# 64-token chunks scored in 64x64 array tiles, y kept transposed, and the attention of 256 tokens traced pair by pair among the MLP of older tokens

## The chip, the cores and the metric

One Trainium2 chip, one of its cores. The metric is the device time in microseconds of one execution, the median of three runs. The profile is one execution's, taken by the hardware profiler.

## What is computed

A gated recurrence (HGRN2) for 4 sequences of 768 tokens with 8 heads of 48 features, then an MLP with the quick GELU on the 3072 tokens. The weights come as float64, all else as float32; everything is computed in fp32.

```python
f = 1 / (1 + exp(-f_logit))                       # [4, 8, 768, 48]
for t in range(768):
    state = f[:, :, t, :, None] * state + einsum('bhd,bhe->bhde', k[:, :, t], v[:, :, t])
    y[:, :, t] = einsum('bhd,bhde->bhe', q[:, :, t], state)
x = y.transpose(0, 2, 1, 3).reshape(3072, 384)
h = x @ w_in                                      # [384, 2048]
out = (h / (1 + exp(-1.702 * h))) @ w_out         # [2048, 384]
```

## The kernel before

`attention` (L136) does a pair of heads of one sequence, all 768 tokens at once, in six chunks of 128. Heads lie on partitions 0 to 47 and 64 to 111. q, k and the gate f are loaded token by token (L144), the gap between the heads is zeroed on GpSimd (L148), and TensorE turns them to [feature, token] (L159). Within a chunk a pair of tokens (s, t) is scored at the one level m = 1, 2, .. 64 at which s lies in the first and t in the second half of a block of 2m tokens. At each level ScalarE copies the second halves of q into a block-diagonal operand `qz` with zeros for the other head (L179), TensorE multiplies it with k for each chunk (L204; the diagonal, L186), VectorE writes the result under a mask into A (L208), and multiplies half of q and half of k by products of gates (L216, L217), which GpSimd makes (L219). Then k is turned back (L228), the states of the chunks are made (L233 into dS, L240), and y is summed from the state's part (L254) and A times v (L258), into `y_nat` [token, feature]. `turn` (L266) transposes that to xT once a sequence's four pairs are done.

`mlp_step` (L276) takes 384 tokens: 16 blocks of h (L284, three matmuls each), sigmoid on ScalarE (L288), product on VectorE (L289), and then three outputs of 16 matmuls (L293), copied (L298) and stored (L300).

`load_weights` (L95) takes 56 pieces. Each comes by DMA as the bits of float64 (L102) and is rounded to fp32 by ten VectorE and three GpSimd instructions (L111 to L130), in which the engines wait for each other twice.

The program traces the pairs of a sequence and then the MLP of the sequence before it. A scheduler then orders each engine's instructions by its own estimate of when they are ready; engines and SP's DMA queue execute in that order.

Of the kernel before, what the change touches and what calls it, by code (L numbers as in the profile page):

```python
# [10 lines left out]
I32 = mybir.dt.int32  # L11
AF = mybir.ActivationFunctionType
ALU = mybir.AluOpType


@with_exitstack
def kernel(
# [24 lines left out]
    C = 128                     # tokens of a chunk  # L42
    NCH = S // C                # chunks of a sequence
    NG = NCH // 2               # chunks of a PSUM bank
# [3 lines left out]
    HC = C // 2  # L48
    NK = DM // P
    NFF = DFF // P  # L50
    TM = S // 2                 # tokens of an MLP step
    FG = 4                      # blocks of d_ff in one tile of g
    assert S % C == 0 and C == P and NCH % 2 == 0 and DM % P == 0 and D <= HS
# [3 lines left out]
    att = ctx.enter_context(tc.tile_pool(name="att", bufs=3))  # L57
    wp = ctx.enter_context(tc.tile_pool(name="wp", bufs=2))
    mlp = ctx.enter_context(tc.tile_pool(name="mlp", bufs=2))
    ps = ctx.enter_context(tc.tile_pool(name="ps", bufs=2, space=bass.MemoryType.PSUM))  # L60
# [3 lines left out]
    # masks[s, l, t']: is s in the first half of the block of 2m tokens whose second half has the t'-th of  # L64
    # the chunk's second-half tokens?
    masks = const.tile([P, len(LEV), HC], F32, name="masks")
    nc.gpsimd.memset(masks, 1.0)
    for l, m in enumerate(LEV):
        blocks = HC // m
        for base, step, chan in ((0, -2 * m, 1), (m - 1, 2 * m, -1)):  # L70
            nc.gpsimd.affine_select(
                out=masks[:, l, :], in_=masks[:, l, :], compare_op=ALU.is_ge, fill=0.0, base=base,
                pattern=[[step, blocks], [0, m]], channel_multiplier=chan,
            )

    # Block-diagonal operands for two heads: the zeros stay, the blocks come and go.
    def diagonal(name, shape, n):
        tiles = [const.tile(shape, F32, name=f"{name}{j}") for j in range(n)]
        for t in tiles:
            nc.gpsimd.memset(t, 0.0)  # L80
        return cycle(tiles)

    qz = diagonal("qz", [P, 2, S // 2], 3)
    stz = diagonal("stz", [P, NCH - 1, 2, D], 2)

# [3 lines left out]
    WI, WO = 256, 192           # columns of a piece of w_in and of w_out  # L89
    pieces = [(w_in[:, c, f:f + WI], moe_w_in[c * P:(c + 1) * P, f:f + WI])  # L90
              for c in range(NK) for f in range(0, DFF, WI)]
    pieces += [(w_out[:, c, e:e + WO], moe_w_out[c * P:(c + 1) * P, e:e + WO])
               for c in range(NFF) for e in range(0, DM, WO)]

    def load_weights(n, dst, src):  # L95
        """One piece of w_in or w_out.  A float64 comes as its bits and is rounded to the nearest fp32."""
        w = dst.shape[1]
        if moe_w_in.dtype == F32:
            nc.sync.dma_start(out=dst, in_=src)
            return  # L100
        bits = wp.tile([P, w, 2], I32, tag="bits", name=f"bits_{n}")
        nc.sync.dma_start(out=bits.rearrange("p c two -> p (c two)"), in_=src.bitcast(I32))  # L102
        lo, hi = bits[:, :, 0], bits[:, :, 1]

        def tmp(tag, dtype=I32, nm=None):
            return wp.tile([P, w], dtype, tag=tag, name=f"{nm or tag}_{n}", bufs=1)
# [3 lines left out]
        e, over, fits = tmp("e"), tmp("over", F32), tmp("fits")  # L110
        ve.tensor_scalar(e, hi, 1, 21, op0=ALU.logical_shift_left, op1=ALU.logical_shift_right)  # L111
        po.tensor_scalar(over, e, 1151.0, 3.0e38, op0=ALU.is_ge, op1=ALU.mult)  # L112
        ve.scalar_tensor_tensor(fits, e, 897.0, over, op0=ALU.is_ge, op1=ALU.is_gt)
        # sign: the sign bit, and the bit by which the low 8 bits of the exponent field turn from one bias
        # to the other; as an fp32 it is 2 or -2.
        sign, t = tmp("sign"), tmp("t")
        ve.tensor_scalar(sign, hi, -(1 << 31), 1 << 30, op0=ALU.bitwise_and, op1=ALU.bitwise_xor)
        po.tensor_tensor(dst, over, sign.bitcast(F32), ALU.mult)
        # t: the value cut off after 23 bits of mantissa.
        ve.tensor_scalar(t, hi, 4, 1, op0=ALU.logical_shift_left, op1=ALU.logical_shift_right)  # L120
        ve.scalar_tensor_tensor(t, lo, 29, t, op0=ALU.logical_shift_right, op1=ALU.bitwise_or)  # L121
        ve.tensor_tensor(t, t, sign, ALU.bitwise_xor)
        # r: the 29 bits after those, times the power of two that they count from.
        r, p2 = tmp("e", nm="r"), tmp("sign", nm="p2")
        rf = r.bitcast(F32)
        ve.tensor_scalar(r, lo, (1 << 29) - 1, None, op0=ALU.bitwise_and)
        ve.tensor_scalar(p2, t, -(1 << 23), None, op0=ALU.bitwise_and)
        ve.scalar_tensor_tensor(rf, r, 2.0 ** -52, p2.bitcast(F32), op0=ALU.mult, op1=ALU.mult)  # L128
        po.tensor_tensor(rf, rf, t.bitcast(F32), ALU.add)  # L129
        ve.copy_predicated(dst, fits, rf)  # L130

    def halves(t, m):
        """[p, block of 2m, half, m] of a tile that holds the S tokens of a sequence."""
        return t.rearrange("p (n two m) -> p n two m", two=2, m=m)

    def attention(b, a, y_nat):  # L136
        i = f"{b}_{a}"
# [1 line left out]
        raw = {}  # L139
        for nm, src in (("f", f_logit), ("q", q), ("k", k), ("v", v)):  # L140
            w = D if nm == "v" else HS
            t = ld.tile([P, NCH, 2, w], F32, tag=f"{nm}raw", name=f"{nm}raw_{i}")
            for h in range(2):
                nc.sync.dma_start(  # L144
                    out=t[:, :, h, :D], in_=src[b, 2 * a + h].rearrange("(c p) d -> p c d", p=C)
                )
            if w > D:
                nc.gpsimd.memset(t[:, :, :, D:], 0.0)  # L148
            raw[nm] = t
        vv = raw["v"]  # L150

# [1 line left out]
        T = {}  # L153
        for nm in "fqk":
            t = att.tile([P, S], F32, tag=f"{nm}T", name=f"{nm}T_{i}")
            for c0 in range(0, NCH, NG):
                pt = ps.tile([P, NG, C], F32, tag="tr", name=f"tr_{nm}_{i}_{c0}", bufs=1)
                for c in range(NG):
                    nc.tensor.transpose(pt[:, c, :], raw[nm][:, c0 + c], ident)  # L159
                nc.scalar.activation(  # L160
                    t[:, c0 * C:(c0 + NG) * C], pt.rearrange("p c t -> p (c t)"),
                    AF.Sigmoid if nm == "f" else AF.Copy,
                )
            T[nm] = t
        Q, K, F = T["q"], T["k"], T["f"]

# [1 line left out]
        # The two heads of a pair share a product: K of both is stationary, and Q moves block by block,  # L168
        # each head's columns with zeros in the other's rows.
        A = att.tile([P, 2 * NCH, C], F32, tag="A", name=f"A_{i}", bufs=2)  # L170

        def blocks(src):
            z = next(qz)
            for h in range(2):
                rows = slice(h * HS, (h + 1) * HS)
                dst = z[rows, h, :src.free_size()]
# [169 lines left out]
```

## Time and profile before

| | |
|---|---|
| runs | 1086.9, 1084.12, 1085.43 us, median 1085.43 |
| profiled execution, first to last instruction | 1085.1 us |
| TensorE (PE) busy | 926.2 us, 4376 matmul records |
| VectorE (DVE) busy | 550.4 us |
| ScalarE (ACT) busy | 327.5 us |
| GpSimd (POOL) busy | 209.2 us |
| granted TensorE clock, mean | 0.909 |
| HBM read, written | 31.46 MB, 4.72 MB |

How to read it: a row of groups has line, engine, operation, output and inputs by the program's names, shapes and count, then the busy time in all and the mean ns of one, then the idle time of the engine before them and what ended it. PEld is the loading of the stationary operand, which goes on beside PE. PE rows count each fp32 matmul twice and a transpose once. Rows of the timeline merge like instructions that follow each other: start, time from the first's start to the last's end, count. A matmul's time includes its way through the array (222 ns for the smallest here), so matmuls that follow each other overlap in it.

### The profile page before, as it was taken

To read this page: it belongs to the slowest core of one execution; us is meant where nothing else is said; L and a number is where in the kernel's file an instruction comes from. 1 tells how busy PE (TensorE), PEld (TensorE's weight loads), DVE (VectorE), ACT (ScalarE), POOL (GpSimd) and SP (SyncE) were. 2 spreads that over 40 slices of the span, in tenths; PEclk is the share of its full clock that TensorE was granted. 3 is DMA by queue.
4 is the path that set the end of the run, shared out by engine and by line. 5 is a ranking of instruction groups with operands and counts; after the bars stand their busy time and mean duration, and the time that the engine had idled before them with its cause. 6 is when DMAs were issued, how large, how long until landed. Compare 5 with 4: busy or idle time off the path is not lost.

```text
span 1085.1 us, 12313 instructions
## 1 busy us (share of the span) xinstructions
PE 926.2 (85%) x4376; PEld 645.8 (60%) x4376; DVE 550.4 (51%) x1264; ACT 327.5 (30%) x705; POOL 209.2 (19%) x354
## 2 busy tenths in 40 slices
PE   4676675856748568999999999999999999999998
PEld 3475564534645446655577776655777766555554
DVE  3878769787777878220267546203575462021120
ACT  3243232412213214120444533204445432021110
POOL 5335143544445442000100110001100000000000
PEclk9768669777867869999999999999999999999999
DMA  9032131311312112000101220001010000000000
GB/s 149 26 68 59 35 73 30 93 31 46 69 29 66 44 40 49 19 7 15 40 12 33 51 52 8 11 15 40 20 26 19 9 8 1 15 7 8 15 0 23
DMA packets 111933, 36.98 MB, mean 34 GB/s; under 512 B 101632, under 2 KB 108800, under 8 KB 111872
## 3 DMA queue, kind: packets, MB, share of 16 engines
q1 hardware_dynamic: 111872, 36.19, 15.0%
q8 instruction: 35, 0.57, 0.2%
q14 instruction: 26, 0.21, 0.1%
HBM read 31.46 MB, written 4.72 MB: 33 GB/s over the span
## 4 chain that ended last, share of the span: by engine, by line
PE 65%; DVE 14%; issue 9%; POOL 8%; ACT 3%; SPq 1%; DMA 0%; POOLq 0%; DVEq 0%; ACTq 0%
PE h L284 20%; PE o L293 19%; PE g L204 12%; PE y L258 4%; POOL over L112 3%; PE gd L186 3%; POOL r L129 3%; DVE A L208 3%; DVE kT L217 2%; PE y L254 2%; ACT qz L179 2%; DVE t L121 1%; POOL tot L219 1%; DVE qT L216 1%; SPq L144 1%
## 5 line engine op out<-in xcount | busy, mean ns | idle before, releaser
L204 PE MATMUL g<-qz,kT 128*128 128x128 f32 x1344 | 204.6, 310 | 100.6 <-DVE kT L217 83.2
L284 PE MATMUL h<-xT,w_in 128*128 128x384 f32 x768 | 276.6, 501 | 0.2 <-DVE g L289 0.2
L204 PEld LDWEIGHTS g<-qz,kT 128*128 128x128 f32 x1344 | 188.5, 219 | 141.3 <-issue 86.8
L293 PE MATMUL o<-w_out,g 128*128 128x384 f32 x768 | 265.8, 491 | 7.7 <-DVE w_out L130 5.1
L289 DVE TENSOR_TENSOR g<-h,sg 128x384 f32<-128x384 f32 x128 | 71.2, 556 | 288.2 <-ACT sg L288 288.2
L179 ACT COPY qz<-qT 64x384 f32<-64x384 f32 (+1 forms) x320 | 155.1, 485 | 193.6 <-DVE qT L216 165.3
L293 PEld LDWEIGHTS o<-w_out,g 128*128 128x128 f32 x768 | 140.3, 191 | 92.9 <-ACT osb L298 6.3
L284 PEld LDWEIGHTS h<-xT,w_in 128*128 128x128 f32 x768 | 141.3, 196 | 75.7 <-issue 1.2
L208 DVE COPY_PREDICATED A<-masks,g 128x384 f32<-128x384 int32 x224 | 152.5, 700 | 43.7 <-PE g L204 40.6
L288 ACT ACTIVATE sg<-h 128x384 f32<-128x384 f32 x128 | 62.9, 491 | 160.2 <-PE h L284 159.1
L112 POOL TENSOR_SCALAR over<-e 128x192 f32<-128x192 int32 (+1 forms) x56 | 58.7, 1048 | 84.1 <-DVE e L111 60.2
L258 PE MATMUL y<-vraw,A 128*128 128x48 f32 x384 | 65.0, 299 | 7.2 <-DVE st L240 7.2
L258 PEld LDWEIGHTS y<-vraw,A 128*128 128x128 f32 x384 | 62.3, 228 | 11.9 <-DVE st L240 6.3
L148 POOL MEMSET fraw<- 128x192 f32 x16 | 4.1, 257 | 331.0 <-PE tr_f L159 329.3
L129 POOL TENSOR_TENSOR r<-r,t 128x192 f32<-128x192 f32 (+1 forms) x56 | 43.0, 767 | 127.0 <-DVE r L128 127.0
L298 ACT COPY osb<-o 128x384 f32<-128x384 f32 x24 | 11.5, 479 | 172.2 <-PE o L293 141.1
L216 DVE TENSOR_TENSOR qT<-qT,tot 128x384 f32<-128x384 f32 x96 | 53.2, 555 | 2.3 <-issue 1.2
L217 DVE TENSOR_TENSOR kT<-kT,tot 128x384 f32<-128x384 f32 x96 | 54.0, 562 | 0.0
L186 PE MATMUL gd<-qz,kT 128*128 128x256 f32 x192 | 50.4, 417 | 0.0
L229 ACT COPY kn<-tk 128x384 f32<-128x384 f32 (+1 forms) x32 | 13.6, 425 | 108.3 <-PE tk L228 108.3
L186 PEld LDWEIGHTS gd<-qz,kT 128*128 128x128 f32 x192 | 39.5, 214 | 6.6 <-ACT kT L160 0.8
L254 PE MATMUL y<-stz,qT 128*128 128x96 f32 x160 | 39.5, 335 | 0.9 <-ACT y_nat L262 0.5
(53 smaller groups left out, 696.4 us busy)
## 6 DMA issues: line engine op xcount, KB each, us to landing
bits<-in_moe_w_in_dram SPq DMA_DIRECT2D x24, 256.0 KB, 2.7
bits<-in_moe_w_out_dram SPq DMA_DIRECT2D x32, 192.0 KB, 2.3
fraw<-in_f_logit_dram SPq DMA_DIRECT2D x32, 144.0 KB, 2.9
qraw<-in_q_dram SPq DMA_DIRECT2D x32, 144.0 KB, 3.0
kraw<-in_k_dram SPq DMA_DIRECT2D x32, 144.0 KB, 3.1
vraw<-in_v_dram SPq DMA_DIRECT2D x32, 144.0 KB, 2.6
out_dram<-osb SPq DMA_DIRECT2D x24, 192.0 KB, 1.9
```

The costliest lines, as they stand in the source:

```text
L112: po.tensor_scalar(over, e, 1151.0, 3.0e38, op0=ALU.is_ge, op1=ALU.mult)
L129: po.tensor_tensor(rf, rf, t.bitcast(F32), ALU.add)
L179: nc.scalar.copy(dst, src[rows])
L186: nc.tensor.matmul(pg[:, 2 * c:2 * c + 2, :], lhsT=K[:, (c0 + c) * C:(c0 + c + 1) * C], rhs=z[:, :, c * C:(c + 1) * C], start=True, stop=True,
L204: nc.tensor.matmul(pg[:, 2 * c:2 * c + 2], lhsT=K[:, (c0 + c) * C:(c0 + c + 1) * C], rhs=z[:, :, (c0 + c) * HC:(c0 + c + 1) * HC], start=T ...
L208: nc.vector.copy_predicated(A[:, 2 * c0:2 * (c0 + NG), :].rearrange("p c (n two m) -> p c n two m", two=2, m=m)[:, :, :, 1, :], mask.unsqu ...
L216: nc.vector.tensor_tensor(qh, qh, t2[:, :, 0:1].broadcast_to((P, n, m)), ALU.mult)
L217: nc.vector.tensor_tensor(kh, kh, t2[:, :, 1:2].broadcast_to((P, n, m)), ALU.mult)
L258: nc.tensor.matmul(py[:, c - c0, h, :], lhsT=A[:, 2 * c + h, :], rhs=vv[:, c, h, :], start=(c == 0), stop=(c == 0 or h == 1),)
L284: nc.tensor.matmul(ph, lhsT=w_in[:, n, ff * P:(ff + 1) * P], rhs=xT[:, n, ts], start=(n == 0), stop=(n == NK - 1))
L289: nc.vector.tensor_tensor(g[-1][:, ff % FG, :], ph, sg, ALU.mult)
L293: nc.tensor.matmul(po, lhsT=g[ff // FG][:, ff % FG, tt * P:(tt + 1) * P], rhs=w_out[:, ff, :], start=(ff == 0), stop=(ff == NFF - 1),)
```

## The change

Attention now takes a unit of 256 tokens and a pair of heads, in chunks of 64 tokens with six levels (m = 1 to 32). A block of 128 tokens has 64 first halves and 64 second halves at every level, so a level's scores for the two heads and the two blocks of a unit are four products of 64 x 64, each in its own quarter of TensorE's array: the head sets the rows, the block the columns. There is no `qz`; instead ScalarE copies the first halves of k into `Kc` (L235). Level 0 takes the diagonal along. One instruction promotes q and k (`promote`, L331), and one masks four levels (L241). The product with v is made level by level, with the v of the first halves loaded in that order (`vl`, 28 DMAs a unit), and gives y as [feature, token] (L256, L306); a DMA carries it into xT (L320), and `turn` is gone. States pass from unit to unit. The scores have one buffer of two banks in PSUM, which dS takes too, and y has one of two banks.

MLP steps are of 256, five times 512 and 256 tokens, and the program is traced so that after each pair of heads of the units to come an eighth (or a quarter) of the MLP step stands. Weights come in 28 pieces with six VectorE and one GpSimd instruction each.

On TensorE, within a sequence's later pairs and among the MLP, stands this before (g are scores, h the MLP's first product):

```order
L204 MATMUL g_1_1_0_3842<-qz_94,kT_1_3808 128x128 x3
L204 MATMUL g_1_1_3_3847<-qz_94,kT_1_3808 128x128 x3
L284 MATMUL h_0_12_4531<-xT_3515,w_in 128x384 x2
L204 MATMUL g_1_2_0_3857<-qz_95,kT_1_3808 128x128 x3
L204 MATMUL g_1_2_3_3862<-qz_95,kT_1_3808 128x128 x3
L284 MATMUL h_0_13_4538<-xT_3515,w_in 128x384 x3
```

and this now, in a pair of unit 3 (sc are scores, y the outputs):

```order
L217 MATMUL sc_1_0_2424<-X_1_2404 64x64 x4
L342 MATMUL h_5_2537<-xT_957,w_in 128x512
L217 MATMUL sc_1_0_2424<-X_1_2404,Kc_1_2423 64x64 x4
L342 MATMUL h_5_2537<-xT_957,w_in 128x512
L256 MATMUL y_1_2469<-A_1_0_2439,vl_2220 48x128 x4
L256 MATMUL y_1_2469<-A_1_0_2439,vl_2220 48x64 x2
L217 MATMUL sc_1_1_2441<-X_1_2404,Kc_1_2423 64x64 x4
L256 MATMUL y_1_2469<-A_1_0_2439,vl_2220 48x64 x2
L256 MATMUL y_1_2469<-A_1_0_2439,vl_2220 48x32x2 x4
L342 MATMUL h_5_2537<-xT_957,w_in 128x512
L217 MATMUL sc_1_1_2441<-X_1_2404,Kc_1_2423 64x64 x4
L342 MATMUL h_6_2544<-xT_957,w_in 128x512
```

Between two levels stands one matmul of h of 512 columns where two or three of 384 stood, and each group between two h is now of small tiles.

In SP's queue near the program's start stands this before (loads of the third pair, and the first pieces of the weights):

```order
L144 DMA vraw_1_343<-in_v_dram 128x6x48 x2
L102 DMA bits_1003<-in_moe_w_in_dram 128x512
L144 DMA fraw_2_555<-in_f_logit_dram 128x6x48 x2
L144 DMA qraw_2_559<-in_q_dram 128x6x48 x2
L102 DMA bits_1025<-in_moe_w_in_dram 128x512
L144 DMA kraw_2_563<-in_k_dram 128x6x48 x2
```

and this now, where the loads of unit 1 (vl) end (bits_847 is the 19th of the 28 pieces):

```order
L166 DMA vl_967<-in_v_dram 16x8x48 x2
L116 DMA bits_825<-in_moe_w_out_dram 128x768
L166 DMA vl_967<-in_v_dram 32x8x48
L116 DMA bits_836<-in_moe_w_out_dram 128x768
L166 DMA vl_967<-in_v_dram 32x8x48 x2
L116 DMA bits_847<-in_moe_w_out_dram 128x768
L166 DMA vl_967<-in_v_dram 32x8x48
```

The loads of a unit, 36 with those of q, k, f and v, stand piece by piece between those of the weights.

The core of the diff:

```diff
-    C = 128                     # tokens of a chunk
+    C = 64
+    G = 128
+    U = 256
...
+    V_HALF = [(1, 0), (1, 1)] + [(m, 0) for m in LEV[1:]]
...
+    def attention(n, a, loaded, xT, x0):
...
+        nc.scalar.copy(view(X, 0, [[2 * U, 2], [1, U]]), pt)
+        nc.vector.tensor_tensor(X[:, 1], X[:, 0], F, ALU.mult)
...
+            sc = ps.tile([P, 2, 512], F32, tag="sc", name=f"sc_{i}_{r}")
+
+            def score(slot, w, lhs, rhs):
+                for g in range(NG):
+                    for h in range(2):
+                        nc.tensor.matmul(
+                            sc[g * HS:(g + 1) * HS, h, slot * 64:slot * 64 + w],
+                            lhsT=lhs(h, g), rhs=rhs(h, g), start=True, stop=True,
+                        )
...
+                if l:
+                    promote(X, tms[l - 1], LEV[l - 1])
+                nc.scalar.copy(
+                    Kc[:, l, :].rearrange("p (n m) -> p n m", m=LEV[l]),
+                    X[:, 2].rearrange("p (n two m) -> p n two m", two=2, m=LEV[l])[:, :, 0, :],
+                )
+                score(slot, 64, lambda h, g: Kc[rows(h), l, g * 64:(g + 1) * 64], tokens(1, LEV[l], 1))
...
+                    prior.append(nc.tensor.matmul(
+                        dst(h, g), lhsT=vl[g * 64:(g + 1) * 64, u, 2 * a + h, :], rhs=rhs(h, g),
+                        start=start, stop=False, skip_group_check=True,
+                    ))
...
+        pd = ps.tile([P, 2, 512], F32, tag="sc", name=f"dS_{i}")
...
+    def promote(X, tm, m):
...
+        qk = view(X, U + m, [[U - m, 2], [2 * m, nb], [1, m]])
+        by = tm.rearrange("p (n two) -> p two n", two=2).unsqueeze(3).broadcast_to((P, 2, nb, m))
+        nc.vector.tensor_tensor(qk, qk, by, ALU.mult)
...
+        a, s = tmp("a"), tmp("s")
+        ve.tensor_scalar(a, hi, 0x7FFFFFFF, None, op0=ALU.bitwise_and)
+        ve.tensor_scalar(s, hi, -(1 << 31), -(1 << 31), op0=ALU.bitwise_and, op1=ALU.bitwise_xor)
+        af = a.bitcast(F32)
+        ve.tensor_scalar(af, af, 2.0 ** 112, 2.0 ** 97, op0=ALU.mult, op1=ALU.max)
+        ve.scalar_tensor_tensor(s, a, 3, s, op0=ALU.logical_shift_left, op1=ALU.bitwise_xor)
+
+        ve.tensor_scalar(a, s, -(1 << 23), None, op0=ALU.bitwise_and)
+        ve.scalar_tensor_tensor(af, lo.bitcast(U32), 2.0 ** -52, af, op0=ALU.mult, op1=ALU.mult)
+        po.tensor_tensor(dst, s.bitcast(F32), af, ALU.add)
...
+    for s, step in enumerate(steps):
...
+        for j, w in enumerate(work):
+            w()
+            want = (j + 1) * len(parts) // len(work)
+            while done < want:
+                next(it)
+                done += 1
```

More of the change, by code (lines that the diff above doesn't have):

```diff
@@ L68 @@
+    nc.gpsimd.memset(full, 1.0)
     for l, m in enumerate(LEV):
-        blocks = HC // m
-        for base, step, chan in ((0, -2 * m, 1), (m - 1, 2 * m, -1)):
+        for base, step, chan in ((0, -m, 1), (m - 1, m, -1)):
             nc.gpsimd.affine_select(
-                out=masks[:, l, :], in_=masks[:, l, :], compare_op=ALU.is_ge, fill=0.0, base=base,
-                pattern=[[step, blocks], [0, m]], channel_multiplier=chan,
-            )
[L77 to L81, printed above, removed]
@@ L83 @@
-    qz = diagonal("qz", [P, 2, S // 2], 3)
-    stz = diagonal("stz", [P, NCH - 1, 2, D], 2)
+                out=full[:, l, :], in_=full[:, l, :], compare_op=ALU.is_ge, fill=0.0, base=base,
+                pattern=[[step, G // m], [0, m]], channel_multiplier=chan,
+            )
+    SLOT_LEVELS = ((0, 0, 0, 1), (2, 3, 4, 5))
+    masks = [const.tile([P, 4, G // 2], F32, name=f"masks{r}") for r in range(2)]
+    for r, levels in enumerate(SLOT_LEVELS):
+        for s, l in enumerate(levels):
+            nc.gpsimd.tensor_tensor(masks[r][:, s, :], full[:, l, :G // 2], full[:, l, G // 2:], ALU.add)
@@ L86 @@
+    raws = [const.tile([P, 3, NG, H, HS], F32, name=f"raw{j}") for j in range(2)]
+    for t in raws:
+        nc.gpsimd.memset(t[:, :, :, :, D:], 0.0)
     w_in = const.tile([P, NK, DFF], F32, name="w_in")
     w_out = const.tile([P, NFF, DM], F32, name="w_out")
[L89 to L93, printed above, removed]
+    WI = 512
@@ L124, in load_weights @@
[L124 to L134, printed above, removed]
@@ L144, in attention @@
                 nc.sync.dma_start(
-                    out=t[:, :, h, :D], in_=src[b, 2 * a + h].rearrange("(c p) d -> p c d", p=C)
+                    out=xT[f0 % P:f0 % P + end - f0, f0 // P, x0:x0 + U], in_=yT[r0:r0 + end - f0, :]
                 )
[L147 to L164, printed above, removed]
@@ L266, in turn @@
[L266 to L277 removed]
+                f0 = end
```

337 lines of the change are left out of this document (189 added, 148 removed).

## The prediction

> **What bounds the kernel now.** I read the page's heads first, then the windows, the waits and the granted clock, to see where TensorE is short of work, and last the timeline, for the price of single instructions.
>
> ```profile
> span 1085.1 us, 12313 instructions
> PEclk9768669777867869999999999999999999999999
> 0.00:440.00 440.00, 295.39 (x1492) 231.91 (x1493) 332.38 (x859) 130.72 (x281) 184.29 (x280) 0.78 0.26 56
> 440.00:1085.00 645.00, 630.78 (x2885) 413.88 (x2883) 218.04 (x406) 196.79 (x424) 24.88 (x74) 1.00 0.08 19
> PE g L204 <- DVE kT L217: 79.8, 38, 6.4
> DVE fits L113 <- POOL over L112: 32.4, 49, 2.2
> ```
>
> The two window rows (columns: PE, PEld, DVE, ACT, POOL busy, granted clock, DMA) say it: two kernels in one. For 440 us VectorE is busy 332 us, TensorE waits for it (79.8 us in the scores' wait alone, which this waits view takes over those 440 us) and runs at 0.78 of its clock; after that TensorE is busy 631 of 645 us at full clock. The next rows are the MLP's two lines (L284, then L293) in the first window, two pieces of the chain, and the masking of the diagonal in that window, three for each pair of heads.
>
> ```profile
> 0.00:440.00 440.00, 47.34 (x98) 19.31 (x98) 0.78 0.26 56
> 0.00:440.00 440.00, 20.35 (x51) 9.72 (x52) 0.78 0.26 56
> 461.15 29.67 PE h L284 x92
> 574.08 2.59 PE gd L186 x12
> L190 DVE TENSOR_TENSOR A<-gd,ident 128x512 f32<-128x512 f32 x24 | 16.4, 687 | 4.0 <-PE gd L186 4.0
> ```
>
> Each fp32 matmul stands twice in the trace; I call each a pass. A pass of 384 columns costs 29.67/92 = 0.3225 us, one of 256 2.59/12 = 0.216, so 0.83 ns a column and 0.429 for 512. A transpose is one pass of 128 columns, 0.11 us. In the first 440 us only 98 + 51 = 149 of 1536 MLP passes are done (48 us of work), and 24/3 = 8 of the 16 pairs of heads, or 24 of 48 pairs of 256 tokens. The other 1387 take 447 us, so the later 24 pairs of 256 tokens, with their turning of x, cost TensorE (645 - 447)/24 = 8.2 us each.
>
> **What the change does to TensorE's steady stage.** The MLP stays nearly what it is: 480 passes of 512 (206 us), 192 of 256 (41 us), 768 of 384 (248 us), 495 us. Scores and outputs become small passes in 64x64 tiles. The nearest thing in the trace is dS, which already runs two 128x64 tiles:
>
> ```profile
> L233 PE MATMUL dS<-vraw,kn x320: 222/222/343, 49.4 to 890.7; 128*64 128x48 f32 x160
> 562.81 0.56 PE L233 MATMUL dS<-vraw,kn 128*64 128x48 f32 x12
> 563.29 0.91 PE L284 MATMUL h<-xT,w_in 128*128 128x384 f32 x2
> 564.14 0.44 PE L233 MATMUL dS<-vraw,kn 128*64 128x48 f32 x8
> ```
>
> Price of a pass: twelve passes take 0.56 us of which the last is 0.222, so they start 0.338/11 = 30 ns apart; with two tiles at once each tile is used every 60 ns. Four tiles, if as independent, give 15 ns; two at a time 30; none overlapping 60. I take 15, since the row shows the two tiles' work overlapping fully, and keep 30 inside the range and 60 for a rival. A rule speaks against this: the Trainium skill gives each matmul some 60 cycles whatever its size, and advises not to take the tiling from a dimension that is small already (TensorEngine Tiling (Array Packing), Instruction Overhead); it puts two starts at least 25 ns apart (TensorE: Matmul & The Clock Gate, Wait — 56ns, not 53.3ns?). By 25 ns the sum below would be 1017 us, an estimate; the dS row's mean of 30 can't tell, and no run here has more than two tiles.
>
> Price of changing the tile size: from the dS burst's start to the next h is 0.48 us, 0.12 more than 12 passes; the two h passes then take 0.85 until the next dS, 0.205 more than 2 x 0.3225. So each dive into small tiles costs 0.325 us beside its passes.
>
> In the new order I counted 419 such dives, 345 of them after the first three units of 256 tokens (12 pairs); those three I treat below. After them stand: MLP, 495 less 46.5 (step 0 and six h), 448.5 us; 288 transposes, 31 us; 345 x 0.325 = 112 us; 5152 small passes, of which 576 have 128 columns and count twice and 528 belong to the state matmuls, which have only two tiles and count twice too: 6256 x 15 ns = 94 us. Sum 685 us for 36 pairs: (685 - 448.5)/36 = 6.6 us a pair. The block-diagonal zeros and the turning of x go, the dives eat most of it.
>
> **Waits there.** Each level now passes VectorE (both promotes in one instruction) and ScalarE (a copy of K) before TensorE can go on.
>
> ```profile
> L216 DVE TENSOR_TENSOR qT<-qT,tot 128x384 f32<-128x384 f32 x96 | 53.2, 555 | 2.3 <-issue 1.2 <-ACT qz L179 0.5
> L190 DVE TENSOR_TENSOR A<-gd,ident 128x512 f32<-128x512 f32 x48 | 32.7, 687 | 13.5 <-PE gd L186 13.5
> L179 ACT COPY qz<-qT 64x384 f32<-64x384 f32 x224 | 116.3, 519 | 191.5 <-DVE qT L216 165.3 <-PE g L204 10.4 <-PE gd L186 7.0
> L179 ACT COPY qz<-qT 64x256 f32<-64x256 f32 x96 | 38.7, 403 | 2.2
> L229 ACT COPY kn<-tk 128x256 f32<-128x256 f32 x16 | 6.0, 373 | 9.8 <-PE tk L228 9.8
> L240 DVE SCALAR_TENSOR_TENSOR st<-st,tot,dS 128x48 f32<-128x48 f32 x64 | 16.7, 261 | 32.8 <-ACT st L238 31.8
> 583.04 0.54 DVE L216 TENSOR_TENSOR qT<-qT,tot 128x384 f32<-128x384 f32 x1
> 583.62 1.04 ACT L179 COPY qz<-qT 64x384 f32<-64x384 f32 x2 [2.31 <-DVE qT L216]
> ```
>
> From 555 at 384 and 687 at 512 a promote of 256 takes 0.42 us; from 519 and 403 a copy of 128 takes 0.29; the hand-over from VectorE to ScalarE is 583.62 - 583.58 = 0.04. So from a level's last score to the next level's first: 0.222 + 0.42 + 0.29 + three hand-overs = 1.05 us. Between them the new order puts one h (two passes of 0.429) or two o (four of 0.3225), and leaving and entering small tiles belongs to that time: 0.86 + 0.325 = 1.19 or 1.62 us. The latency is covered, by little in the h half. What is not: behind the mask product (0.69) stands a promote that the next scores need, and the four state updates (0.261 each) make 1.04 us before the state matmuls. dS takes the scores' two banks, so the next pair's first scores wait for the states too; an h stands ahead of them. With gelu products (0.69) in VectorE's queue I put 1 us a pair, 36 us, and 2 us (an estimate) for each of five new MLP steps, whose third h waits for the last pair's y by way of a copy, SP's queue and a DMA: 10 us. If the h's cover were gone the price would be some 3 us a pair more.
>
> SP gets 36 loads for each unit:
>
> ```profile
> 4.49 1.73 SPq L144 DMA_DIRECT2D vraw<-in_v_dram  x2
> ```
>
> 768 descriptors take SP 0.87 us; a unit has 15360, so some 17 us, and ten small DMAs that carry y to x, in a stage that gives it over 60 us: hidden, as long as SP doesn't stand at one of the ten.
>
> **The first three units.** There is no MLP to cover anything, and the weights must be converted. New code has six VectorE instructions a piece in place of ten, and one GpSimd step in place of a round trip.
>
> ```profile
> L128 DVE SCALAR_TENSOR_TENSOR r<-r,p 128x192 f32<-128x192 int32 x32 | 11.6, 361 | 0.0
> L128 DVE SCALAR_TENSOR_TENSOR r<-r,p 128x256 f32<-128x256 int32 x24 | 11.1, 463 | 0.5
> L111 DVE TENSOR_SCALAR e<-bits 128x192 int32<-128x192 int32 x32 | 8.3, 258 | 0.0
> L111 DVE TENSOR_SCALAR e<-bits 128x256 int32<-128x256 int32 x24 | 7.4, 306 | 17.0 <-DMA bits<-in_moe_w_in_dram 17.0
> 9.30 0.90 PE L159 MATMUL tr_f<-ident,fraw 128*128 128x128 f32 x3 [9.30 <-POOL fraw L148]
> 1077.84 4.03 PE L293 MATMUL o<-w_out,g 128*128 128x384 f32 x12
> ```
>
> By these slopes (1.6 and 0.75 ns an element) a two-input instruction takes 0.87 us at 512 and 0.67 at 384, a one-input one 0.50 and 0.40; a piece of w_in 3.7 us, of w_out 2.9; 12 + 16 pieces 92 us. A pair needs VectorE for seven 0.42, two 0.69 and four 0.261: 5.4 us. Unit 1's last loads stand in SP's queue behind the 19th piece, whose buffer waits for VectorE: so its first pair can't end before 19 pieces (65 us), five pairs (27 us) and 16 gelu products (7 us) are through VectorE, from about 11.5 us on (GpSimd's set-up is about as long as the 9.3 us now), with some 13 us idle in the uncovered chains of unit 0 (an estimate, from 12 us a chain against 5.4 of work in the first of them): 124 us. Then three pairs with the other nine pieces, 47 us. Unit 2's four pairs run on their chain: five levels of promote, copy, hand-overs and scores (1.25 each), two mask products and what follows (2.5), transpose, copy and dS (1.5), states (1.1), the first scores (0.7): 12 us a pair, 48 us. Together 219 us; 185 if VectorE is kept busy throughout, 240 if the chains and the conversions add up.
>
> **The sum.** 219 + 685 + 46 + 3.2 (from the last matmul's end to the span's) = 953 us, against a span of 1085.1; the median of the runs is 1085.4, so the span can be taken for the time. Cross-check: at the point where before has spent 440 us, the new kernel has done as much after 219 + 12 x 7.8 = 313 (7.8 is 6.6 and the waits' 46/36); the later 24 pairs gain little (7.8 against 8.2 us).
>
> **The rivals.**
> Two at a time (0.20): passes start 30 ns apart whatever the number of tiles. For it: no row shows four tiles, and the dS row's mean is 30. 94 us more: 1047. The Trainium skill's rule, above, is this rival in a milder form.
> Cover too thin (0.13): one h between levels is too short with copies and gelu queued ahead, 3 us a pair: 953 + 108 = 1061. Against it: 1.19 us stands against 1.05.
> Cheap start (0.10): conversions and chains fit into each other fully, 185 us, and dives overlap the waits: 885.
> No tile overlap (0.07), the one on the slower side, and the case in which the change does not do what it says: the passes of different row halves follow each other at 60 ns: 6256 x 45 ns = 282 us more, 1235. It decides from 15 + 132/6256 = 36 ns a pass. Against it is the dS row.
>
> My forecast has 0.50: 953 us, by itself 915 to 990. The range leaves out the last rival and the ends: 870 to 1065. A measurement of this kernel can tell 0.3% from no change. Faster 0.91, the first four cases but for their tails; same 0.01; slower 0.08, the last rival and a little of the third.
>
> **What would show it.** Right: scores' passes some 15 ns apart in a burst; 0.3 us lost at each dive; the fourth unit begun near 219 us; TensorE busy from there at clock 1.00; VectorE's busy time near 420 us. Wrong: passes 30 ns or more apart; waits of TensorE for ScalarE's K copy of over 2 us a pair; a low clock in the later stage; TensorE waiting for DMAs of v or y.

## The result, and the profile after

The changed kernel takes 965.29 us (median of 4 runs, 962.35 to 966.6) where the kernel before takes 1086.16 (median of 4): a ratio of 0.889, 95% interval 0.886 to 0.892. The profiled execution spans 964.9 us.

The head of the page after, and the windows of TensorE's thin and full stage (columns as before: span of the window, then PE, PEld, DVE, ACT, POOL busy, granted clock, DMA share):

```profile
span 964.9 us, 20905 instructions
PE 879.1 (91%) x8672; PEld 473.7 (49%) x8672; DVE 385.3 (40%) x904; ACT 240.8 (25%) x617; POOL 126.0 (13%) x345
PEclk9997987655699999999999999999999999999999
...
0.00:182.00 182.00, 126.34 (x1344) 78.66 (x1344) 117.00 (x284) 36.10 (x97) 58.45 (x105) 0.89 0.51 121
182.00:252.00 70.00, 47.73 (x628) 28.70 (x620) 20.84 (x52) 14.26 (x40) 6.48 (x24) 0.57 0.32 57
252.00:965.00 713.00, 705.02 (x6724) 366.30 (x6714) 247.44 (x568) 190.41 (x480) 61.10 (x216) 0.99 0.25 46
```

The thin stage ends at 252 us and not at 440; from there TensorE is busy 705 of 713 us. The 70 us before are unit 2, with a granted clock of 0.57.

The longest wait of TensorE's matmuls in the first 252 us, and there the wait of VectorE's promotes (us in all, times, longest):

```profile
PE sc L217 <- ACT Kc L235: 25.8, 32, 1.3
DVE X L331 <- PE sc L217: 31.4, 33, 2.3
```

Where scores waited for VectorE (79.8 us before) they now wait for ScalarE's copy of K, and VectorE's promotes wait for the scores: a chain, and no engine that is full.

How much of the 120 us came from where? The MLP passes of the first 252 us, by line (L342 is h, L352 is o), and the start of units 3 and 11:

```profile
0.00:252.00 252.00, 38.56 (x108) 21.33 (x108) 0.80 0.45 103
0.00:252.00 252.00, 32.81 (x64) 12.79 (x64) 0.80 0.45 103
252.13 0.69 PE L187 MATMUL tf<-ident,raw 128*128 128x128 f32 x2
808.64 0.44 PE L187 MATMUL tf<-ident,raw 128*128 128x128 f32 x2
```

Between 252.1 and 808.6 lie 32 pairs and four MLP steps of 512 tokens, each 96 passes of 0.429 us and 128 of 0.3225, 82.5 us: (556.5 - 330)/32 = 7.1 us a pair beside the MLP, where before took 8.2. By the prediction's prices the MLP passes of the first 252 us are 46.5 us of work, much what before had done in 440 (149 passes, 48 us). Before had also done 24 pairs; the new kernel has 12 and needs 12 x 7.1 = 85 us for as many. So it stands at 252 + 85 + 2 = 339 us where before stood at 440: by these prices some 101 us come from the front, and the other 19 from the later stage.

### The profile page after: what moved, and what is told of

Read it like the earlier page. It is cut to its first block, busy times and chain, and to the rows that moved or that the text cites. A ratio compares the mean times of both kernels' runs of the same rounds, so it can differ in the third digit from the quotient of the medians.

```text
span 964.9 us, 20905 instructions
## 1 busy us (share of the span) xinstructions
PE 879.1 (91%) x8672; PEld 473.7 (49%) x8672; DVE 385.3 (40%) x904; ACT 240.8 (25%) x617; POOL 126.0 (13%) x345
## 4 chain that ended last, share of the span: by engine, by line
PE 83%; DVE 7%; SPq 3%; ACT 3%; POOL 2%; issue 2%; DMA 1%; DVEq 0%; ACTq 0%
PE o L352 28%; PE h L342 27%; PE sc L217 9%; PE y L256 7%; PE y L306 3%; PE tqk L192 3%; PE dS L281 2%; PE tk L274 2%; PE tf L187 2%; DVE X L331 2%; POOL w_out L135 1%; SPq L163 1%; DVE A L241 1%; DVE s L131 1%; DVE a L134 1%
## 5 line engine op out<-in xcount | busy, mean ns | idle before, releaser
L352 PE MATMUL o<-w_out,g 128*128 128x384 f32 x768 | 306.0, 517 | 8.7 <-POOL w_out L135 8.7
L342 PE MATMUL h<-xT,w_in 128*128 128x512 f32 (+1 forms) x672 | 307.7, 571 | 0.8 <-DMA xT<-yT 0.6
L352 PEld LDWEIGHTS o<-w_out,g 128*128 128x128 f32 x768 | 131.2, 193 | 67.4 <-POOL w_out L135 10.5
L331 DVE TENSOR_TENSOR X<-X,tot 128x256 f32<-128x256 f32 x240 | 105.1, 438 | 131.3 <-PE sc L217 130.9
L235 ACT COPY Kc<-X 128x128 f32<-128x128 f32 x240 | 71.8, 299 | 295.6 <-DVE X L331 295.6
L342 PEld LDWEIGHTS h<-xT,w_in 128*128 128x128 f32 x672 | 113.5, 194 | 38.2 <-issue 21.4
L217 PE MATMUL sc<-X,Kc 48*64 48x64 f32 x1920 | 93.0, 258 | 27.1 <-ACT Kc L235 26.9
L256 PEld LDWEIGHTS y<-A,vl 64*48 64x48 f32 x2688 | 70.6, 133 | 75.2 <-DVE A L241 45.6
L203 POOL TENSOR_TENSOR tot<-F 128x128 f32<-128x128 f32 x48 | 19.6, 409 | 665.7 <-ACT F L188 665.6
L256 PE MATMUL y<-A,vl 64*48 64x64 f32 (+1 forms) x2688 | 91.1, 251 | 14.6 <-DVE A L241 14.1
L347 DVE TENSOR_TENSOR g<-h,sg 128x512 f32<-128x512 f32 (+1 forms) x112 | 68.4, 612 | 86.4 <-ACT sg L346 86.4
L241 DVE TENSOR_TENSOR A<-sc,masks 128x512 f32<-128x512 f32 x96 | 66.4, 691 | 74.5 <-PE sc L217 74.5
L346 ACT ACTIVATE sg<-h 128x512 f32<-128x512 f32 (+1 forms) x112 | 60.0, 536 | 102.6 <-PE h L342 97.5
L296 DVE SCALAR_TENSOR_TENSOR st<-st,tot,dS 128x48 f32<-128x48 f32 x176 | 46.5, 264 | 66.6 <-PE dS L281 61.1
L194 DVE TENSOR_TENSOR X<-X,F 128x256 f32<-128x256 f32 x48 | 20.4, 425 | 122.5 <-ACT X L193 122.4
L203 POOL TENSOR_TENSOR tot<-tot 128x64 f32<-128x64 f32 (+4 forms) x240 | 63.4, 264 | 18.6
L306 PEld LDWEIGHTS y<-X,st 48*48 48x48 f32 x704 | 27.1, 130 | 39.8 <-DVE st L296 28.2
```

The source lines that it names most:

```text
L203: nc.gpsimd.tensor_tensor(tn, t2[:, :, 0], t2[:, :, 1], ALU.mult)
L217: nc.tensor.matmul(sc[g * HS:(g + 1) * HS, h, slot * 64:slot * 64 + w], lhsT=lhs(h, g), rhs=rhs(h, g), start=True, stop=True,)
L235: nc.scalar.copy(Kc[:, l, :].rearrange("p (n m) -> p n m", m=LEV[l]), X[:, 2].rearrange("p (n two m) -> p n two m", two=2, m=LEV[l])[:, :, ...
L241: nc.vector.tensor_tensor(At, sc[:, :, :256].rearrange("p h (s t) -> p h s t", t=64), masks[r].unsqueeze(1).broadcast_to((P, 2, 4, 64)), A ...
L256: prior.append(nc.tensor.matmul(dst(h, g), lhsT=vl[g * 64:(g + 1) * 64, u, 2 * a + h, :], rhs=rhs(h, g), start=start, stop=False, skip_gro ...
L296: nc.vector.scalar_tensor_tensor(st[:, c, :], before, D64[:, c:c + 1], d, op0=ALU.mult, op1=ALU.add)
```

## The experiments

The ratio of the changed kernel (after) to before is 0.889 [0.886, 0.892]; each run below has its own ratio to before.

### 1. Do the four tiles run side by side?

Edit: the outputs are issued tile by tile.

```diff
         def add(u, rhs, dst, start=False):
-            for h in range(2):
-                for g in range(NG):
-                    prior.append(nc.tensor.matmul(
+            todo.append((u, rhs, dst, start))
...
+        for h in range(2):
+            for g in range(NG):
+                for u, rhs, dst, start in todo:
+                    prior.append(nc.tensor.matmul(
```

> The 28 output matmuls of a pair are issued tile by tile (seven in one 64x64 tile, then seven in the next) in place of level by level over four tiles; the arithmetic is the same. Theory (four tiles run side by side, so 14 ns a pass is 56 ns of a tile divided by four, and TensorE sets the time of the later 36 pairs): the 56 passes of a pair, 64 counted by 64 columns, go from 14 to some 56 ns, 2.7 us a pair, 97 us over 36 pairs, and some 15 in the first three units: 1077 us. Rival A (a pass starts 14 ns after the last whatever the tile): 965. Rival B (the chain of levels, not TensorE, sets a pair's 17.1 us, and the outputs fill waits): at most half of it, 1010 or less.

1092.42 us, 1.007 [1.005, 1.008]: 127 us more than after, and no faster than before. A burst of outputs in after (two columns ahead of the engine: start and length in us), and the same outputs tile by tile:

```profile
302.40 0.67 PE L256 MATMUL y<-A,vl 64*48 64x64 f32 x32
```

```profile
315.16 2.92 PE L271 MATMUL y<-A,vl 64*48 64x64 f32 x50
```

With 0.25 us for the last pass, 31 starts in 0.42 us are 14 ns apart, 49 in 2.67 us 55 ns. The theory of four tiles holds and Rival A falls: passes that follow each other in one tile wait for it, passes in four tiles wait only for their own tile's last one. The 55 ns are close to what 64 columns take at the long matmuls' 0.83 ns each, 53 ns. That the passes of one tile also add to the same columns of y doesn't explain it: o's sixteen matmuls, each of two passes, add to one place too and take no more than their columns (0.32 us for 384). Rival B falls too. The pairs from unit 3 to unit 10 take 19.6 us in place of 17.4, some 80 us for 36; the other 47 arise in the first three units (unit 3 starts at 298 us in place of 252), where I had 15.

### 2. What does a change of tile shape cost?

Edit: the middle matmul of each h becomes two of 64 columns.

```diff
-                nc.tensor.matmul(
-                    ph, lhsT=w_in[:, n, ff * P:(ff + 1) * P], rhs=xT[:, n, :T], start=(n == 0), stop=(n == NK - 1)
-                )
+                for c in range(0, P, P // 2 if n == 1 else P):
+                    w = P // 2 if n == 1 else P
+                    nc.tensor.matmul(
+                        ph[c:c + w], lhsT=w_in[:, n, ff * P + c:ff * P + c + w], rhs=xT[:, n, :T],
+                        start=(n == 0), stop=(n == NK - 1)
+                    )
```

> The middle one of an h's three matmuls is issued as two matmuls of 64 columns of weights each; the arithmetic is the same. The order then has 1015 changes of tile shape in place of 838. Theory (a way into another tile shape and back costs 0.33 us of TensorE, and TensorE sets the time): 177/2 x 0.33 = 29 us, so 994 us, if the two column tiles overlap fully. Rival A (a change of shape costs nothing, the gap seen at a dive has another cause): 965. Rival B (the chain of levels sets the time, TensorE has room): 970 or less. If the two column tiles do not overlap, 83 us more than the theory's 994.

1035.06 us, 0.952 [0.945, 0.959]: 70 us more than after, between the theory's 994 and its case without overlap. Both happen in one trace:

```profile
276.12 2.13 PE L344 MATMUL h<-xT,w_in 128*64 128x512 f32 x6
278.19 0.58 PE L217 MATMUL sc<-X 48*64 48x128 f32 x16
...
280.03 1.07 PE L344 MATMUL h<-xT,w_in 128*64 128x512 f32 x2
281.04 0.58 PE L256 MATMUL y<-A,vl 64*48 64x128 f32 x12
...
282.07 2.13 PE L344 MATMUL h<-xT,w_in 128*64 128x512 f32 x4
```

In the first row four half passes and two full ones take 2.13 us; in the last, where the other half stood ahead of the outputs, two half passes and two full ones take the same 2.13. So halves that follow each other run side by side. Up to the scores the first row takes 2.07 us: 0.86 for the full ones, 0.86 for the halves, and 0.35 that is left for two changes. Where scores stand between the halves (56 of the 80 h of 512 tokens in the new order) one half alone takes as long as a full matmul, 0.86 us more: 48 us. With 29 us for the changes that makes 77, against 70 measured; the trace doesn't say where the other 7 are hidden, and the run by itself doesn't part the two terms. Rivals A and B fall. Pairs beside o, which isn't split, stay at 17.1 us; those beside h go to 20.4.

### 3. Does the gain hang on tracing pair by pair?

```diff
-            want = (j + 1) * len(parts) // len(work)
+            want = 0
```

> The attention of all pairs of a step is traced ahead of the MLP of the step before, not pair by pair; the arithmetic is the same. Theory (TensorE's work sets the time as long as some MLP pass stands between two levels; the work is the same): some pairs at a step's end lose their cover and run on their chain, 5 of them at 5 us each in the worst case, 965 to 990. Rival (the pair-by-pair order is what the gain hangs on: the cover is used up early in a step, and half of the 36 pairs run uncovered with 5 us or more idle each): 1050 or more.

961.5 us, 0.884 [0.879, 0.890], not to be told from after: tracing pair by pair, a part of the change, gains nothing here. The scheduler itself puts MLP passes between the levels; seven pairs of a step take some 15.5 us and the rest of the MLP follows densely, so that the step takes as long. The rival falls. The windows of this run, of about two steps each, show a full TensorE as in after:

```profile
252.00:530.00 278.00, 273.56 (x2853) 140.71 (x2850) 103.69 (x242) 79.45 (x202) 25.14 (x96) 0.98 0.36 64
530.00:805.00 275.00, 273.72 (x2863) 140.01 (x2862) 103.61 (x240) 79.07 (x200) 25.00 (x96) 1.00 0.24 47
```

### 4. What sets the first 252 us? The conversion and the loads

Four runs, each with one edit. First the conversion's six VectorE instructions and GpSimd's add become one copy:

```diff
-        a, s = tmp("a"), tmp("s")
...
-        po.tensor_tensor(dst, s.bitcast(F32), af, ALU.add)
+        ve.tensor_copy(dst, hi.bitcast(F32))
```

> Leaves out the rounding of float64 weights: one VectorE copy of the high word in place of six VectorE instructions and a GpSimd add for each of 28 pieces, so the weights are wrong. Theory (unit 1 is set by the ring of VectorE's six instructions, GpSimd's add and the single buffer between them, 3.6 to 4.0 us a piece, on whose w_out pieces TensorE's o matmuls stand in order): unit 1 falls from 101.5 us to the 70 that unit 2 takes on its chain, unit 0 stays near 69: 930 us. Rival A (SP's queue and the DMA of the loads set unit 1): 955 or more. Rival B (conversions set units 0 and 1 both, by all 78 us that they take of VectorE): 890.

966.16 us, 0.889 [0.884, 0.894]: nothing gained. My theory fell, and so did Rival B; Rival A's time came out, and the run with early loads below tests its reason.

Then two buffers for a, with s in the result's place:

```diff
-            return wp.tile([P, w], I32, tag=tag, name=f"{tag}_{n}", bufs=1)
+            return wp.tile([P, w], I32, tag=tag, name=f"{tag}_{n}", bufs=2)
-        a, s = tmp("a"), tmp("s")
+        a, s = tmp("a"), dst.bitcast(I32)
```

> The conversion keeps s in the place of the result, so that a can have two buffers: VectorE's next piece need not wait for GpSimd's add of the last; same instructions, same arithmetic. Theory (the ring through the single buffer paces unit 1): each piece's ring loses the 0.8 to 1.1 us that VectorE waits for the add, some 17 to 25 us over 28 pieces: 944 us. Rival (VectorE's work or the transfers pace it, the wait is hidden): 965.

969.57 us, 0.892 [0.890, 0.895]: nothing gained; the theory fell again.

Then unit 1's loads ahead of the weights:

```diff
+    ahead[1] = load_unit(1)
     for n, piece in enumerate(pieces_in + pieces_out):
```

> Unit 1's loads are traced ahead of the weights' loads, all else the same. Theory (unit 1 is paced by the conversion ring, not by SP's order): within 8 us of 965, later weights and earlier tokens cancelling. Rival (the loads of unit 1, queued on SP behind the pieces, hold its first pair back and make the gap of 42 us between its second and third pair): 925 to 945.

965.4 us, 0.889 [0.887, 0.892]: nothing gained, as expected, though the ring that I gave as the reason is not it. The place of unit 1's loads in SP's queue doesn't set the front either, so Rival A of the run without conversion loses its reason as far as SP's order goes.

And the old conversion (`load_weights` and its pieces of 256 and 192 columns as before the change):

```diff
-    WI = 512
+    WI, WO = 256, 192
...
+        ve.copy_predicated(dst, fits, rf)
```

> The old conversion of the weights (56 pieces, ten VectorE instructions and three of GpSimd each) in the new kernel. Theory (the conversion's VectorE time paces units 0 and 1): the old one took about twice the VectorE time, some 80 us more, all of it in front of unit 2: 1040 us, two thirds of the way back to the old kernel. Rival (the tiles make the gain, the conversion is hidden): 965 to 980.

1038.68 us, 0.957 [0.954, 0.959]: 73 us more. The time is the theory's; its reason, VectorE's time, isn't shown by it, since pieces, instructions and round trips to GpSimd came back together. The old conversion is too long to hide, the new one hides, and what is saved beyond it is worth nothing in this program. Of the 120 us of the whole change 73 are gone with the old conversion; with it the rest of the change gains 47. How much of that the tiles, the shorter chunks and the units of 256 give each wasn't run.

The run without conversion shows what takes the time there: TensorE's rows around unit 1's first pair, and the first scores of the pairs after it (the last row is unit 3).

```profile
101.84 5.88 PE L333 MATMUL h<-xT,w_in 128*128 128x256 f32 x26
107.65 0.33 PE L247 MATMUL y<-A,vl 64*48 64x64 f32 x8
107.91 3.29 PE L333 MATMUL h<-xT,w_in 128*128 128x256 f32 x14
111.03 5.97 PE L343 MATMUL o<-w_out,g 128*128 128x384 f32 x18
...
134.93 0.33 PE L208 MATMUL sc<-X 48*64 48x128 f32 x1
151.78 0.92 PE L208 MATMUL sc<-X 48*64 48x128 f32 x16 [1.53 <-DVE X L185]
169.11 0.92 PE L208 MATMUL sc<-X 48*64 48x128 f32 x16 [1.52 <-DVE X L185]
186.45 0.92 PE L208 MATMUL sc<-X 48*64 48x128 f32 x16 [1.52 <-DVE X L185]
...
256.50 0.92 PE L208 MATMUL sc<-X 48*64 48x128 f32 x16 [1.52 <-DVE X L185]
```

From 97 to 133 us the order has nearly the whole MLP of unit 0 in one block, with unit 1's outputs strewn into it; then seven pairs follow bare, 17.3 us each (151.78 to 169.11). So the front of that run is a sum: 11 us of set-up, 12 pairs of 17.3 and a block of some 33, 252 us. The scheduler gave that run another order on TensorE. In after mostly h stands as a block, and o stands among unit 1's later pairs, where it waits for converted weights (from 81 to 182 us):

```profile
PE o L352 <- POOL w_out L135: 8.7, 8, 2.4
```

So the run shows that nothing is gained by leaving the conversion out; it doesn't show that the conversion holds nothing up in after's own order. With early loads w_out is converted from 165 to 233 us, TensorE waits 23.8 us for converted weights, and unit 3 still starts no later. Why three different orders end so near each other wasn't shown. Unit 3's first scores, where after and the three edits without the old conversion differ by less than 6 us:

| kernel | after | without conversion | two buffers | early loads | old conversion |
|---|---|---|---|---|---|
| unit 3's first scores, us | 257.3 | 256.5 | 259.5 | 254.2 | 323.6 |

### 5. Can the MLP cover unit 2?

```diff
-    steps = [[0]] + [[n, n + 1] for n in range(1, NALL - 1, 2)] + [[NALL - 1]]
-    TM = 2 * U
+    steps = [[n] for n in range(NALL)]
+    TM = U
```

> Twelve MLP steps of 256 tokens in place of one, five of 512 and one. Theory (from unit 3 on TensorE is full, unit 2 is set by its uncovered chain, half of it at a granted clock of 0.57): unit 2 now has the MLP of unit 1 between its levels, 22 us of idle TensorE there are used; 12 more dives 4 us and five more step starts cost 5 to 10 us: 950 us. Rival (shorter h passes are too thin a cover: 0.65 us or 1.3 in place of 0.43 x 3 between levels, so all later pairs wait): 990 or more.

926.84 us, 0.854 [0.852, 0.856]: 38 us better than after, where I expected 15. The windows of this run:

```profile
179.00:254.00 75.00, 72.28 (x776) 45.20 (x773) 27.98 (x72) 20.93 (x59) 6.46 (x24) 0.92 0.38 66
254.00:924.00 670.00, 663.41 (x7025) 426.61 (x7023) 246.54 (x628) 189.18 (x541) 57.15 (x216) 1.00 0.23 47
```

Unit 2 is no shorter, but TensorE is busy 72.3 of 75 us in it (47.7 of 70 in after), at a clock of 0.92 in place of 0.57: a whole MLP step is done there, and 43 us less are left after it. The rival falls: shorter h passes cover the levels as well.

### 6. What makes a bare pair 17.3 us long?

Unit 2 in after, from dS of one pair to the first scores of the next, and then a level:

```profile
215.08 0.68 PE L281 MATMUL dS<-vn,kn 64*64 64x48 f32 x16 [0.46 <-ACT kn L276]
215.70 0.69 PE L187 MATMUL tf<-ident,raw 128*128 128x128 f32 x2
215.90 1.16 DVE L296 SCALAR_TENSOR_TENSOR st<-st,tot,dS 128x48 f32<-128x48 f32 x4 [2.73 <-PE dS L281]
...
218.32 0.67 PE L306 MATMUL y<-X,st 48*48 48x64 f32 x8
218.92 0.47 PE L192 MATMUL tqk<-ident,raw 128*128 128x128 f32 x1
219.03 0.76 ACT L315 COPY yT<-y 48x256 f32<-48x256 f32 x2 [2.17 <-PE y L306]
219.81 0.58 ACT L193 COPY X<-tqk 128x512 f32<-128x512 f32 x1
220.43 0.42 DVE L194 TENSOR_TENSOR X<-X,F 128x256 f32<-128x256 f32 x1 [3.36 <-ACT X L193]
220.91 0.92 PE L217 MATMUL sc<-X 48*64 48x128 f32 x16 [1.52 <-DVE X L194]
```

```profile
208.66 0.49 PE L217 MATMUL sc<-X,Kc 48*64 48x64 f32 x8 [0.55 <-ACT Kc L235]
209.32 0.43 DVE L331 TENSOR_TENSOR X<-X,tot 128x256 f32<-128x256 f32 x1 [1.04 <-PE sc L217]
209.78 0.30 ACT L235 COPY Kc<-X 128x128 f32<-128x128 f32 x1 [1.17 <-DVE X L331]
210.13 0.49 PE L217 MATMUL sc<-X,Kc 48*64 48x64 f32 x8 [0.97 <-ACT Kc L235]
```

A level takes 1.47 us. And from the next pair's first transpose to its first scores pass 5.2 us, with nothing of the former pair's levels beside them: tk (K turned back) has the one bank that tf and tqk need, and dS the two of the scores. The edit puts both elsewhere:

```diff
-        pt = ps.tile([P, NG, P], F32, tag="tr", name=f"tk_{i}")
+        pt = py[:, :, 384:]
-        pd = ps.tile([P, 2, 512], F32, tag="sc", name=f"dS_{i}")
+        pd = py[:, :, 256:384]
```

> The turned K (tk) and dS go into unused columns of y's two banks in place of the banks that they share with the transposes of F, Q, K and with the scores; same instructions, same arithmetic. So the next pair's transposes and first scores need not wait for this pair's tk and dS. Theory (the first three units are 12 pairs of 17.3 us on one chain, of which some 7 us, from the last mask product to the next first scores, are there because of the shared banks, plus one stretch of MLP of 33 us; from unit 3 on TensorE sets the time): pairs of some 11 us in units 0 and 2, unit 1 then held by the conversion, unit 3 begun near 207 and not 252 us, later pairs 17.1 as before: 920 us (905 to 935). Rival A (something else of fixed length, loads or conversions, holds unit 3 to 250 us, as it seemed to in the runs without conversion and with early loads): 960 or more. Rival B (the chain's length is that of the levels at a low clock): 950 or more.

932.8 us, 0.860 [0.858, 0.862]: 32 us better than after, inside the theory's range; both rivals fall. Part of y's sums is lost in this run and in the next two (the last run keeps them), so only their times are read. The window from 182 us to about unit 3, and unit 3's first scores, right behind the former pair's tk (now in y's tile, line L274):

```profile
182.00:224.00 42.00, 29.52 (x456) 19.07 (x454) 15.12 (x39) 10.10 (x29) 4.75 (x18) 0.60 0.45 84
...
228.29 0.67 PE L256 MATMUL y<-A,vl 64*48 64x64 f32 x32
228.89 0.44 PE L274 MATMUL y<-ident,X 128*128 128x128 f32 x2
229.26 0.45 PE L217 MATMUL sc<-X 48*64 48x128 f32 x6
```

Unit 3 stands at 229.3 in place of 257.3; unit 2's pairs take 13.6 us on average (first scores at 174.9 to 229.3) where I had 11. The clock is still 0.60: the low clock doesn't hinder the gain, and how much of a pair it costs wasn't tried by itself, nor was tk's bank apart from dS's.

> Both: the banks apart and MLP steps of one unit. Theory: from unit 2 on TensorE is full, and idle are the set-up of 11 us, half of unit 0 and the end of unit 1, 35 to 45 us; 860 us of TensorE work as in the kernel of one-unit steps: 895 us (885 to 910). Rival (both edits use the same idle time): 915 to 925, no better than the better one alone.

908.08 us, 0.837 [0.836, 0.838]: a shorter time than with either edit alone, so the rival falls; it is 13 us above the theory's 895, inside its range.

> Banks apart, one-unit steps, unit 1's loads ahead of the weights' and two buffers in the conversion. Theory (with the chain shortened the conversion ring and the order on SP are next in unit 1): 10 to 20 us better than banks apart with one-unit steps, 880 us. Rival (they stay hidden as they were alone): the same 895.

939.84 us, 0.866 [0.864, 0.868]: 32 us worse than without the two additions; neither theory nor rival. VectorE and TensorE from 180 us to this kernel's unit 3:

```profile
180.00:277.00 97.00, 88.51 (x798) 53.68 (x797) 52.67 (x128) 20.77 (x58) 17.88 (x28) 0.97 0.47 104
```

VectorE is busy 52.7 us in these 97; in the kernel of one-unit steps 28.0 in 75. The weights come behind unit 1's loads and their conversion now reaches beyond 180 us: from 81 us to unit 3 TensorE waits 29 us for converted weights, without the two additions 12. The early loads are what shifts it: by themselves they move the last conversion to 233 us, while with two buffers by themselves it is at 159. By themselves they cost nothing, though; what each of the two additions costs in this kernel wasn't run.

> The version of banks apart and one-unit steps that keeps y whole: dS goes into unused columns of y's two banks without a start flag of its own, and tk takes the scores' tile in turn, so that only its copy to kn stands ahead of the next pair's first scores. In the two runs with the banks apart the start flags of tk and dS made the state matmuls overwrite the scores' share of y, so only their times can be read. Theory (the flags carry no time, and tk's turn in the scores' tile costs the next pair less than 2 us where there is no MLP to cover it, nothing where there is): 908 to 918 us. Rival (the short time of the run with both came from the sums that were lost): 927, that of one-unit steps alone, or more.

Last, tk and dS moved in another way, on the one-unit steps:

```diff
+        pt = ps.tile([P, 2, 512], F32, tag="sc", name=f"tk_{i}")[:, :, :P]
+        pd = py[:, :, 256:384]
-                        rhs=vn[c * C:(c + 1) * C, g, 2 * a + h, :], start=True, stop=True,
+                        rhs=vn[c * C:(c + 1) * C, g, 2 * a + h, :], start=False, stop=False, skip_group_check=True,
```

913.23 us (5 runs), 0.841 [0.839, 0.842]: the best version that computes all of y, 52 us better than after. It lies in the theory's range, and the rival (927 or more) falls.

```profile
0.00:180.00 180.00, 124.52 (x1309) 78.23 (x1309) 112.98 (x283) 35.75 (x98) 61.63 (x111) 0.85 0.52 121
180.00:250.00 70.00, 67.24 (x822) 43.83 (x819) 28.45 (x73) 20.62 (x59) 5.00 (x18) 1.00 0.35 65
```

TensorE is full from 180 us on; what is still idle are 55 us of the first 180.

## Why the prediction was right, and where not

The forecast was 953 us; 965.29 was measured. The step that carries the gain, the price of a pass, was right; that the sum came within 13 us of the time is in part luck, as two errors below cancel.

**Price of a pass: right.** 15 ns forecast, 14 measured (experiment 1). "Two at a time" and "no tile overlap" fall. The Trainium skill's 25 ns between two starts (TensorE: Matmul & The Clock Gate, Wait — 56ns, not 53.3ns?) does not hold for passes in four tiles: the trace has 14. (Its estimate of 1017 us, 1016 by the sum's own terms, is 51 us above the measured time; since other terms were off by 33 and 38 us, the time alone would hardly tell.) "No tile overlap" was no idle rival: with the outputs alone made to queue for their tiles, the kernel is no faster than before.

**Price of a dive: right.** 0.325 us forecast. Rows of after in the full stage:

```profile
298.41 0.34 PE L217 MATMUL sc<-X,Kc 48*64 48x64 f32 x8
298.69 1.13 PE L342 MATMUL h<-xT,w_in 128*128 128x512 f32 x2
299.74 0.34 PE L217 MATMUL sc<-X,Kc 48*64 48x64 f32 x8
300.02 1.13 PE L342 MATMUL h<-xT,w_in 128*128 128x512 f32 x2
```

From h to h 1.33 us, less 0.86 for its passes and 8 x 14 ns for the scores': 0.36. Experiment 2 agrees in size, within the 7 us that its two terms leave open.

**Waits in the full stage: too dear.** I put 46 us there. TensorE is idle 8 us of 713, and an h between two levels covers them, as the same rows show (no wait is noted at either burst). "Cover too thin" falls. The sum from unit 3 on was 685 + 46 + 3 = 734 and is 713: dives 345 x 0.035 = 12 us more, waits 38 less; the other 5 us these rows don't place. (By the loops of the kernel the small passes there are 5136, not 5152, which is 0.2 us.)

**The first three units: too cheap.** 219 us forecast, 252 measured, and this is the step that failed, in two terms: unit 2, 22 of the 33 us, and units 0 and 1, the other 11. Unit 2 was to take 12 us a pair; it takes 17.5 (187.3 to 257.3 in first scores). My sum had the levels, the mask products, dS and the states, and let the next pair's F, Q and K be turned beside them; the shared banks forbid it (experiment 6), 5.2 us less the 1.1 that I had for the states. Another 0.2 us was missing at each of five levels, 0.15 of it from bursts of 0.49 us where the full stage has 0.34. Unit 1 was to be held by the conversions and SP's queue. The time came out near (its first pair's end at 124 forecast, the second pair's first scores at 129.2), but that was luck: without any conversion, or with unit 1's loads early, unit 3 starts within about 3 us of the same time (experiment 4), so neither holds the front by itself. What the sum gave no time of its own is TensorE's MLP work in the front, the 46.5 us that it took off the later stage: without conversion some 33 us of it stand as a block beside which no chain goes on. What holds unit 1 in after's own order stays open. "Cheap start" falls too.

The two errors, 33 us too little in the front and 21 too much after it, cancel in part. The sum's cross-check had put the equal point at 313 us, and it is 339.

**VectorE** is busy 385 us where I had some 420: the conversion's six lines take 78 us where the slopes gave 92, and the rest these rows don't place.

## What to carry to other kernels

Small matmuls are cheap only in groups that fill all four tiles in turn, and each change of shape costs a third of a microsecond, so count the dives as well as the passes. Where independent work fills the engine, long chains cost nothing; at the start, where it doesn't, look which buffers tie one item's end to the next one's beginning, and let some of the filling work be there early. Before a long piece of work is made shorter, it is worth one run that leaves it out altogether: here that run gained nothing. But compare the order of instructions in that run too, since the scheduler may have made another one.

## What the runs showed of the hardware that was not expected

- Two passes in the same 64x64 tile start 55 ns apart with 64 columns each; in four tiles, 14 ns on average. In after's burst at 302.40 us four passes, one for each tile, start 7 ns apart, and from the second round on each tile's next pass starts some 56 ns after its last.
- Two column halves of one matmul run side by side when they follow each other (four half passes and two full ones take 2.13 us, as do two half passes and two full ones) and not with scores between them: a half alone takes as long as the whole.
- In the three runs with tk and dS written under start flags into unused columns of y's banks, part of y's sum was lost; in the last run, with tk elsewhere and dS without the flag, it was kept. The Trainium skill says why: a start flag clears the written marks of the whole bank on the partitions that it touches (PSUM — Partial Sum Buffer, The four PSUM rules). These runs agree; they don't separate tk's part from dS's, and that the lost part is the scores' share is read from that rule, not measured.
